# A fixed opening order laid out anew: fourth unit's scores earlier, two units' exponentials in a row, keys and values loaded per unit

## The chip, the core and the metric

The kernel runs on one core of one Trainium2 chip. A core has five engines that work side by side, each through its own queue in order: TensorE (matrix products; PE in the profile, PEld its weight loads), VectorE (DVE), ScalarE (ACT), GpSimd (POOL) and SyncE (SP), which here issues most DMA transfers. The metric is the device time of one execution in microseconds (us). The kernel before has a median of 1154.69 us over three runs (1153.79 to 1156.12).

## What is computed

Attention in chunks over 4 batches, 8 heads, 768 positions and 64 features per head, followed by two dense blocks over the 3072 tokens of 512 features, all in float32:

```python
for c in range(nc):                       # chunks of 32 queries
    k_full = concat(mem_k, k[c_start-16 : c_end+8])
    v_full = concat(mem_v, v[c_start-16 : c_end+8])
    a = exp(scale * q_c @ k_full.T - max)
    out[c] = (a / (sum(a) + 1e-9)) @ v_full
x = out as 3072 x 512
h = x @ w_in                               # 512 -> 2048
x = maximum(0.01 * h, h) @ w_out           # 2048 -> 512
return ((x @ w_a) * (x @ w_b)) @ w_out2    # 512 -> 1536 -> 512
```

## The kernel before

**Attention units.** Attention is cut into 24 units of 128 tokens (`UT`), six per batch. A unit goes through: `a_scores` (32 small products on TensorE, line 267), `a_max` (VectorE: row maxima, and for most units the subtraction), `a_exp` (ScalarE; for units 2 and 3, `by_scalar`, eight instructions that also sum), `a_soft2` (VectorE: division by the sum), `a_turn_mm` and `a_turn_copy` (transposes on TensorE, copies on ScalarE), `a_pv` (32 small products with V on TensorE, line 375) and `a_out` (ScalarE writes a rounded part `xh`, VectorE the remainder `xl`, the two halves of the split that gives float32 accuracy). Keys and values come by `k_load` and `v_load` (lines 251 and 259), two DMA transfers of 256 KB per unit, four buffers each.

**Weights.** `w_in` and `w_out` come as 16 column blocks and 16 row blocks. `order` is the list in which they are prepared: (0,0), (1,0), (2,0), (0,1), (3,0), (1,1), (4,0), (2,1) and so on, where (f,0) is a block of `w_in` and (f,1) one of `w_out`. Each entry goes through `Weights`: `load` (DMA of 512 KB), `bias` (ScalarE, line 103), `join` (three VectorE instructions, lines 113, 116 and 119), `cast` (ScalarE, line 173) and `low` (VectorE, line 182). `step` does one join, the biases of two later entries and the low part of the entry before.

**First dense block.** Tokens are taken in six blocks of 512. For a column block f, `mm1` (lines 412 to 414, tile `h`) multiplies x by (f,0), ScalarE applies the leaky rectifier (`g`) and rounds (`gh`), VectorE takes the remainder (`gl`); `mm2` (lines 532 to 536, tile `a`) multiplies by (f,1), two column blocks behind. For the first token block the first three column blocks (`LEAD`) are done on the first 256 tokens only (units 0 and 1), so that TensorE can begin before units 2 and 3 are ready; from f = 3 on all 512 tokens are taken.

**The order.** `InOrder` (line 31) wraps the engines: each instruction emitted through `pe`, `dve`, `act` or `sp` is put behind the one emitted before it on the same engine. So the opening, from the first load to the end of `first_items` (line 580), is an order written out by hand, in the sequence of the source. At its end `e.on = False` is set for all four wrappers, and from there on the framework's scheduler orders instructions by priority and its own estimate of when they are ready; instructions emitted through `nc.scalar` and the like are free from the start. In the profile the instructions of the written order carry line 44 or 47, the wrapper's; the free ones carry their own lines, and they may slip in among the others.

## Time and profile before

| what | us |
|---|---|
| median of three runs | 1154.69 |
| the profiled execution | 1154.32 |
| its span, first to last instruction | 1152.5 |
| TensorE busy in it | 1134.1 |
| VectorE busy | 665.4 |
| ScalarE busy | 441.7 |

The page's busy line gives each engine's share of the span, the table of stretches the same for parts of it, with the granted TensorE clock (1.00 is the level of 2.4 GHz, 0.50 that of 1.2 GHz) and the share of the time in which the 16 DMA engines worked. In a timeline a row has start, duration, engine, source line, operation, the tiles written and read, shapes, and in brackets the idle time of the engine before it with what ended it.

### The profile page before, as it was taken

What the parts mean: (1) busy time and instruction counts of PE and PEld (TensorE: products, weight loads), DVE (VectorE), ACT (ScalarE), POOL (GpSimd) and SP (SyncE); (2) the same over time, 40 slices, a digit from 0 to 9 for tenths busy, and PEclk for the clock granted to TensorE, in tenths of its full rate; (3) what the DMA queues carried; (4) which work ended last, traced back from release to release, by engine and by line L of the source; (5) the groups of instructions that cost most, each with busy time, mean ns of one, the idle gap of its engine ahead of it and who ended that gap; (6) DMA issues with size and microseconds to landing.
All of it is one profiled execution on the core that took longest, in us unless ns stands there. A gap on an engine that the chain in (4) does not pass through costs nothing.

```text
span 1152.5 us, 16036 instructions
## 1 busy us (share of the span) xinstructions
PE 1134.1 (98%) x6344; PEld 938.6 (81%) x6344; DVE 665.4 (58%) x1233; ACT 441.7 (38%) x734; POOL 6.3 (1%) x16
## 2 busy tenths in 40 slices
PE   6899999999999999999999999999999999999998
PEld 6678888888888888888888888888888888888887
DVE  6899489889979834545114433475433465433443
ACT  5787564556455534325223222241222232122210
POOL 2000000000000000000000000000000000000000
PEclk9999999999999999999999999999999999999999
DMA  9977899998999845336248335355544344443413
GB/s 325 354 264 279 308 341 322 317 354 300 330 339 333 298 164 182 111 114 215 92 146 314 144 128 201 128 227 220 208 148 163 146 148 187 185 166 142 186 64 110
DMA packets 68299, 250.67 MB, mean 217 GB/s; under 512 B 7297, under 2 KB 8705, under 8 KB 62849
## 3 DMA queue, kind: packets, MB, share of 16 engines
q1 hardware_dynamic: 67920, 249.33, 60.3%
q8 instruction: 50, 0.82, 0.3%
q10 hardware_dynamic: 304, 0.33, 0.1%
q14 instruction: 25, 0.20, 0.1%
HBM read 200.34 MB, written 49.28 MB: 217 GB/s over the span
## 4 chain that ended last, share of the span: by engine, by line
PE 94%; DVE 0%; DVEq 0%; issue 0%
PE h L412 7%; PE a L532 7%; PE a L536 7%; PE a L535 7%; PE h L414 7%; PE h L413 7%; PE o L925 6%; PE o L927 6%; PE o L926 6%; PE A L860 4%; PE A L859 4%; PE A L858 4%; PE C L858 3%; PE C L860 3%; PE C L859 3%; PE pv L385 2%
## 5 line engine op out<-in xcount | busy, mean ns | idle before, releaser
L412 PE MATMUL h<-xh,w 128*128 128x512 f32 (+1 forms) x384 | 152.1, 396 | 3.1 <-ACT w L47 3.1
L532 PE MATMUL a<-gh,w 128*128 128x512 f32 (+1 forms) x392 | 150.7, 385 | 0.9 <-DVE w L182 0.9
L535 PE MATMUL a<-gl,w 128*128 128x512 f32 (+1 forms) x392 | 150.4, 384 | 0.0
L536 PE MATMUL a<-gh,w 128*128 128x512 f32 (+1 forms) x392 | 150.4, 384 | 0.0
L413 PE MATMUL h<-xl,w 128*128 128x512 f32 (+1 forms) x384 | 149.0, 388 | 0.0
L414 PE MATMUL h<-xh,w 128*128 128x512 f32 (+1 forms) x384 | 148.9, 388 | 0.0
L430 DVE TENSOR_TENSOR gl<-g,gh 128x512 fp32r<-128x512 f32 (+1 forms) x96 | 65.4, 682 | 105.8 <-ACT gh L429 105.6
L925 PE MATMUL o<-w,cl 128*128 128x512 f32 x288 | 112.1, 389 | 0.0
L927 PE MATMUL o<-w,ch 128*128 128x512 f32 x288 | 112.0, 389 | 0.0
L926 PE MATMUL o<-w,ch 128*128 128x512 f32 x288 | 112.0, 389 | 0.0
L514 ACT ACTIVATE g<-h 128x512 f32<-128x512 f32 (+1 forms) x96 | 56.5, 589 | 126.3 <-PE h L414 125.5
L872 ACT COPY u<-A 128x512 f32<-128x512 f32 x72 | 42.3, 588 | 142.2 <-PE A L860 142.2
L412 PEld LDWEIGHTS h<-xh,w 128*128 128x128 f32 x384 | 72.5, 189 | 18.7 <-ACT w L47 3.2
L532 PEld LDWEIGHTS a<-gh,w 128*128 128x128 f32 x392 | 73.7, 188 | 16.3 <-DVE w L182 1.3
L880 DVE TENSOR_TENSOR ga<-u,C 128x512 f32<-128x512 f32 x36 | 24.8, 688 | 106.9 <-ACT u L872 77.7
L536 PEld LDWEIGHTS a<-gh,w 128*128 128x128 f32 x392 | 73.6, 188 | 14.5
L535 PEld LDWEIGHTS a<-gl,w 128*128 128x128 f32 x392 | 73.7, 188 | 14.5
L414 PEld LDWEIGHTS h<-xh,w 128*128 128x128 f32 x384 | 72.4, 189 | 14.8
L859 PE MATMUL A<-cl,wab 128*128 128x512 f32 x216 | 84.1, 389 | 0.0
L858 PE MATMUL A<-ch,wab 128*128 128x512 f32 x216 | 84.0, 389 | 0.0
L860 PE MATMUL A<-ch,wab 128*128 128x512 f32 x216 | 84.0, 389 | 0.0
L413 PEld LDWEIGHTS h<-xl,w 128*128 128x128 f32 x384 | 72.6, 189 | 14.1 <-DVE xl L47 0.3
(138 smaller groups left out, 1918.7 us busy)
## 6 DMA issues: line engine op xcount, KB each, us to landing
wab<-wab SPq DMA_DIRECT2D x36, 1792.0 KB, 7.4
w<-wod SPq DMA_DIRECT2D x116, 512.0 KB, 5.2
raw<-w SPq DMA_DIRECT2D x68, 512.0 KB, 6.9
k<-kl SPq DMA_DIRECT2D x48, 256.0 KB, 5.4
v<-vl SPq DMA_DIRECT2D x48, 256.0 KB, 5.4
wab<-pwb SPq DMA_DIRECT2D x12, 1024.0 KB, 7.7
wab<-pwa SPq DMA_DIRECT2D x12, 768.0 KB, 7.2
wod<-w SPq DMA_DIRECT2D x16, 512.0 KB, 6.1
```

The lines of the kernel that those rows point to most:

```text
L412: pe.matmul(ps, w[1], x[0], start=first, stop=False)
L413: pe.matmul(ps, w[0], x[1], start=False, stop=False)
L414: pe.matmul(ps, w[0], x[0], start=False, stop=last)
L532: pe.matmul(ps, slot[:, 1, c], gh[:, t], start=f == 0 and o == 0, stop=False, **kw)
L535: pe.matmul(ps, slot[:, 0, c], gl[:, t], start=False, stop=False, **kw)
L536: pe.matmul(ps, slot[:, 0, c], gh[:, t], start=False, stop=f == NF1 - 1 or (o == HALF and f == LEAD - 1), **kw)
L858: nc.tensor.matmul(ps, w[:, 1, i, c], hi[:, kc], start=first and kc == 0, stop=False, **kw)
L859: nc.tensor.matmul(ps, w[:, 0, i, c], lo[:, kc], start=False, stop=False, **kw)
L860: nc.tensor.matmul(ps, w[:, 0, i, c], hi[:, kc], start=False, stop=kc == HC - 1, **kw)
L925: nc.tensor.matmul(o, cl[:, q], w[:, 0, :], start=k == 0, stop=False)
L926: nc.tensor.matmul(o, ch[:, q], w[:, 1, :], start=False, stop=False)
L927: nc.tensor.matmul(o, ch[:, q], w[:, 0, :], start=False, stop=k == NCH - 1)
```

## The change

Keys and values of a unit come in one transfer of 512 KB each, with two buffers instead of four. The first unit's keys are issued first on SP, and the query halves of the first two units are spread over the queues of ScalarE and SP. `W1.load(7)` becomes `W1.load(6)` ahead of the fourth unit's values. In the written order: the cast of entry 1 goes behind the bias of entry 2; `a_scores(3)` comes from behind the first `mm1` and bias group to right behind `a_pv(1)`; `a_exp(3)` follows `a_exp(2)` with one bias between; the first `mm1` group is emitted ahead of all that `first_items` does, its `g` far later, behind both units' turned copies; both turns come together; `g1`, `join` of entry 5 and `g2` come behind the low part of entry 4; `a_turn_mm(3)` uses the `ps_a` pool. ScalarE stays in the written order through the first `W1.step()` of the loop.

```diff
--- before.py
+++ after.py
@@ -228,9 +228,9 @@
         while loaded[0] < min(upto, NU):
             u = loaded[0]
             if u < len(qs):
-                eng = act if u < 2 else sp
-                sp.dma_start(out=qs[u][0:64, 0:CH, :], in_=q_l[u, 0:64])
-                eng.dma_start(out=qs[u][64:128, CH:2 * CH, :], in_=q_l[u, 64:128])
+                first, second = ((act, sp), (sp, act), (sp, sp))[min(u, 2)]
+                first.dma_start(out=qs[u][0:64, 0:CH, :], in_=q_l[u, 0:64])
+                second.dma_start(out=qs[u][64:128, CH:2 * CH, :], in_=q_l[u, 64:128])
             else:
                 t = ap_.tile([P, CH, 16], F32, tag="qr", name="qr", bufs=2)
                 sp.dma_start(out=t, in_=q_l[u])
@@ -249,26 +249,27 @@
         copy(qb[64:128, :, CH:2 * CH], t[64:128])
 
     def k_load(upto):
-        while loaded[1] < min(upto, 2 * NU):
-            u, cp = divmod(loaded[1], 2)
-            t = ap_.tile([P, 512], F32, tag="k", name="k")
-            sp.dma_start(out=t, in_=k_l[u, cp])
-            kt[u, cp] = t
+        while loaded[1] < min(upto, NU):
+            u = loaded[1]
+            t = ap_.tile([P, 2, 512], F32, tag="k", name="k", bufs=2)
+            sp.dma_start(out=t, in_=k_l[u].rearrange("c p n -> p c n"))
+            kt[u] = t
             loaded[1] += 1
 
     def v_load(upto):
-        while loaded[2] < min(upto, 2 * NU):
-            u, cp = divmod(loaded[2], 2)
-            t = ap_.tile([P, 512], F32, tag="v", name="v")
-            sp.dma_start(out=t, in_=v_l[u, cp])
-            vt[u, cp] = t
+        while loaded[2] < min(upto, NU):
+            u = loaded[2]
+            t = ap_.tile([P, 2, 512], F32, tag="v", name="v", bufs=2)
+            sp.dma_start(out=t, in_=v_l[u].rearrange("c p n -> p c n"))
+            vt[u] = t
             loaded[2] += 1
 
     def a_scores(u):
         qb = q_of(u)
         s = ps_s.tile([P, 8, 64], F32, tag="s", name="s")
+        kk = kt.pop(u)
         for cp in range(2):
-            k = kt.pop((u, cp))
+            k = kk[:, cp]
             for hp in range(4):
                 for cpar in range(2):
                     o = (2 * cp + cpar) * 4 + hp
@@ -375,8 +376,9 @@
     def a_pv(u, pool, tag):
         pt = PT[u % 2]
         o = pool.tile([P, KC, UT], F32, tag=tag, name="pv")
+        vv = vt.pop(u)
         for cp in range(2):
-            v = vt.pop((u, cp))
+            v = vv[:, cp]
             for pair in range(2):
                 for cpar in range(2):
                     for hpar in range(2):
@@ -440,13 +442,13 @@
     W1 = Weights(order)
 
     x_tiles(("x", 0))
+    k_load(1)
     q_load(1)
     k_load(2)
     q_load(2)
-    k_load(4)
     act.dma_start(out=ident, in_=id_l)
     W1.load(1)
-    v_load(2)
+    v_load(1)
     W1.load(2)
     q_load(3)
 
@@ -459,11 +461,11 @@
     a_scores(0)
     a_scores(1)
     fill(6)
-    k_load(6)
-    v_load(4)
+    k_load(3)
+    v_load(2)
     W1.load(3)
     q_load(4)
-    k_load(8)
+    k_load(4)
     W1.load(5)
     a_max(0)
     a_exp(0)
@@ -477,8 +479,8 @@
     a_turn_copy(0, (1,))
     W1.bias(2)
     a_pv(0, ps_h, "h")
-    v_load(6)
-    W1.load(7)
+    v_load(3)
+    W1.load(6)
     W1.join(0)
     a_soft2(1)
     W1.join(1)
@@ -487,16 +489,18 @@
     a_scores(2)
     a_turn_copy(1)
     W1.join()
+    W1.cast(1)
+    W1.low(1)
+    W1.bias(3)
+    a_max(2)
     W1.cast(2)
-    W1.low(1)
-    a_max(2)
-    W1.bias(3)
     a_pv(1, ps_h, "h")
-    v_load(8)
+    v_load(4)
     W1.load(11)
     a_out(1, ("x", 0), UT)
     W1.low(2)
     a_exp(2)
+    a_scores(3)
 
 
     acc = {}
@@ -572,54 +576,51 @@
         if u > 3:
             q_place(u + 1, nc.scalar.copy)
         q_load(u + 3)
-        k_load(2 * u + 6)
+        k_load(u + 3)
 
     def load_v(u):
-        v_load(2 * u + 6)
+        v_load(u + 3)
 
     def first_items():
         parts = [items[f][2] for f in range(LEAD)]
+        h0 = mm1_pe(0, parts[0])
+        a_max(3)
+        a_soft2(2)
+        W1.bias(4)
+        a_exp(3)
         W1.join()
-        a_soft2(2)
-        h0 = mm1_pe(0, parts[0])
-        g0 = mm1_act(*h0)
-        W1.bias(4)
-        W1.cast(3)
-        W1.bias(5)
-        a_scores(3)
-        a_max(3)
-        W1.low(3)
+        h1 = mm1_pe(0, parts[1])
         a_turn_mm(2, ps_a, "a")
         a_turn_copy(2)
-        a_exp(3)
-        h1 = mm1_pe(0, parts[1])
+        W1.cast(3)
+        a_soft2(3)
+        a_turn_mm(3, ps_a, "a")
         a_pv(2, ps_s, "s")
         W1.join()
+        W1.low(3)
+        a_turn_copy(3)
+        g0 = mm1_act(*h0)
+        W1.bias(5)
+        W1.low(4)
+        h2 = mm1_pe(0, parts[2])
+        a_pv(3, ps_s, "s")
         W1.join()
-        W1.cast(4)
-        a_soft2(3)
-        W1.low(4)
         a_out(2, ("x", 0), 2 * UT)
+        mm2(0, parts[0], g0)
+        a_out(3, ("x", 0), 3 * UT)
+        W1.low(5)
         load_qk(2)
         W1.load(12)
         load_v(2)
         W1.load(13)
         g1 = mm1_act(*h1)
-        h2 = mm1_pe(0, parts[2])
-        a_turn_mm(3, ps_s, "s")
-        mm2(0, parts[0], g0)
-        a_turn_copy(3)
-        W1.cast(5)
         W1.bias(6)
         W1.join()
-        a_pv(3, ps_s, "s")
-        W1.low(5)
-        a_out(3, ("x", 0), 3 * UT)
         g2 = mm1_act(*h2)
         load_qk(3)
         load_v(3)
         W1.low(6)
-        for e in (pe, dve, act, sp):
+        for e in (pe, dve, sp):
             e.on = False
         return [(0, parts[1], g1), (0, parts[2], g2)]
 
@@ -796,6 +797,7 @@
         if first:
             W1.load(2 * f + 14)
             W1.step()
+            act.on = False
         behind.append((bi, parts, mm1(bi, parts)))
         if first:
             W1.step()
```

## Rows read from the trace of the kernel before

**Rows 1.** The page's busy line: us, share of the span, instructions.
```profile
PE 1134.1 (98%) x6344; PEld 938.6 (81%) x6344; DVE 665.4 (58%) x1233; ACT 441.7 (38%) x734; POOL 6.3 (1%) x16
```
**Rows 2.** Stretches: length, busy PE, PEld, DVE, ACT, POOL, clock, DMA share, GB/s.
```profile
8.00:20.00 12.00, 10.66 (x162) 9.79 (x160) 10.30 (x21) 6.17 (x11) 0.00 (x0) 1.00 1.04 339
20.00:38.00 18.00, 12.38 (x168) 11.03 (x164) 15.36 (x32) 17.16 (x56) 0.00 (x0) 1.00 0.97 375
38.00:66.00 28.00, 26.24 (x145) 21.10 (x145) 25.46 (x49) 20.39 (x32) 0.00 (x0) 0.94 0.77 277
66.00:112.00 46.00, 46.00 (x313) 37.79 (x314) 44.90 (x87) 36.21 (x60) 0.00 (x0) 1.00 0.88 310
```
**Rows 3.** TensorE's waits: two rows from 8 to 66 us, then after 66.
```profile
PE h L412 <- ACT w L47: 3.1, 1, 3.1
...
PE a L532 <- DVE w L182: 0.9, 2, 0.5
...
PE a L532 <- DVE w L182: 0.5, 1, 0.5
```
**Rows 4.** Timeline of the first 10 us: scores behind the keys, first maximum.
```profile
7.36 3.17 PE L47 MATMUL s<-k,qs 128*64 128x64 f32 x48 [0.23 <-DMA k<-kl]
...
8.56 0.69 DVE L47 TENSOR_REDUCE m<-s 128x8 f32<-128x512 f32 x1 [6.62 <-PE s L47]
```
**Rows 5.** Tile k: issue to landing, first unit's keys, then the fourth unit's.
```profile
DMA to landing us min/median/max: 4.4/4.7/5.1
...
DMA to landing us min/median/max: 6.1/6.1/6.1
```
**Rows 6.** Timeline from 15 to 31 us, some rows.
```profile
15.45 1.00 SPq L47 DMA_DIRECT2D k<-kl  x2
...
22.39 0.68 DVE L47 TENSOR_TENSOR w<-z,w 128x512 fp32r<-128x512 f32 x1
...
24.02 2.00 PE L47 MATMUL s<-k,qs 128*64 128x64 f32 x32
24.13 0.39 ACT L47 ACTIVATE g<-h 128x256 f32<-128x256 f32 x1
...
27.93 0.32 ACT L47 ACTIVATE p<-s,m 128x64 f32<-128x64 f32 x1
...
30.27 0.66 ACT L47 CAST w<-z 128x512 fp32r<-128x512 f32 x1
```
**Rows 7.** Timeline from 31 to 39 us: ScalarE's, VectorE's, TensorE's rows.
```profile
31.53 0.72 ACT L103 ACTIVATE raw<-raw 128x512 f32<-128x512 f32 x1
...
32.42 0.63 PE L47 MATMUL pT<-id,p 128*128 128x128 f32 x4 [1.59 <-DVE p L47]
...
33.08 1.18 ACT L47 COPY pt<-pT 64x512 f32<-64x512 f32 x2 [0.54 <-PE pT L47]
...
35.52 0.43 DVE L47 TENSOR_SCALAR z<-raw 128x512 int32<-128x512 int32 x1 [1.72 <-ACT raw L47]
...
37.41 0.68 DVE L47 SCALAR_TENSOR_TENSOR z<-raw,z 128x512 int32<-128x512 int32 x1
38.01 0.69 DVE L47 TENSOR_TENSOR w<-z,w 128x512 fp32r<-128x512 f32 x1
38.13 0.62 ACT L47 CAST w<-z 128x512 fp32r<-128x512 f32 x1 [0.15 <-DVE z L47]
```
**Rows 8.** Timeline from 38 to 45 us: first 512-wide products and the copies.
```profile
38.84 0.77 PE L412 MATMUL h<-xh,w 128*128 128x512 f32 x1 [3.14 <-ACT w L47]
...
43.20 0.28 PE L532 MATMUL a<-gh,w 128*128 128x256 f32 x1
...
44.56 1.11 ACT L248 COPY qz<-qr 64x512 f32<-64x512 f32 x1
44.63 0.40 PE L412 MATMUL h<-xh,w 128*128 128x512 f32 x1
```
**Rows 9.** A stretch, columns as in rows 2.
```profile
38.61:42.02 3.41, 3.18 (x7) 2.46 (x8) 3.41 (x9) 1.92 (x4) 0.00 (x0) 0.50 0.96 347
```

## The prediction

> **What bounds the kernel now.** I read the page's busy line first, then a table of stretches, then TensorE's waits, then the rows of the start in order of time. The busy line gives TensorE 1134.1 of 1152.5 us [rows 1], so 18.4 us of idle time is all that a new order can win. The stretches say where it lies: from 66 to 112 us TensorE is busy 46.00 of 46.00 us, while from 20 to 38 us it is busy 12.38 of 18.00 with ScalarE at 17.16 and VectorE at 15.36, and from 38 to 66 us 26.24 of 28.00 with VectorE at 25.46 [rows 2]. TensorE's waits after 66 us hold one entry, 0.5 us [rows 3], ahead of the group that starts at 65.96, on that very edge. So the end moves with the moment at which TensorE passes 66 us, and behind it nothing can be won. The start is an alternation of ScalarE and VectorE in a fixed order; its dearest wait is 3.1 us ahead of the first 512-wide product [rows 3]. I call that product step 3, its successor step 4 (TensorE's `h` groups), and the second-layer groups between them a1 and a2. I call the n-th entry of `order`, counted from 0, piece n. Step 3 needs piece 4, a1 piece 5, step 4 piece 6, a2 piece 7.
>
> **Prices.** VectorE takes 0.43 + 2 x 0.68 = 1.79 us for the three instructions that join a piece and 0.69 for its low part [rows 7]. ScalarE takes 0.72 for a bias and 0.62 for a cast [rows 7], 0.39 for `g` of a half block and as much for `gh`, 0.8 in all, and 30.27 - 27.93 = 2.34 for the eight exponentials of a unit [rows 6]. None of these is added or removed; all are moved.
>
> **Keys and values per unit.** The halves of the first unit's keys landed 4.4 and 5.1 us after their issue, and the scores went on at 7.36 behind the second one [rows 4, 5]. VectorE's first maximum came at 8.56 [rows 4]. Now one transfer of 512 KB is issued first, and no score starts before all of it is there. Full scores cost 2.00 us [rows 6], half of which used to run before 7.36. If the whole lands at 6.6 us (0.7 before the second half did, since one 128 KB transfer less is ahead of it) the maximum starts at about 8.75, 0.2 later. The bounds are 5.1 us (the first half's 4.4 us behind an issue at 0.74) and 8.0 us (0.7 behind the second half), so the shift lies between -1.3 and +1.6. I book it at nothing: the next step waits for a later transfer and has 1.3 us to cover it. Later units load the same bytes as early as before, where TensorE waits for no transfer.
>
> **Fourth unit's scores behind the second's products with V.** Before, they ran at 24.02, after the first product; now they stand ahead of it. They need the fourth unit's keys: two transfers issued from 15.45 to 16.45 that took 6.1 us each, so the second landed at about 22.2 [rows 5, 6]. TensorE, free after the second unit's products, waits until then and finishes at 24.3. That costs TensorE nothing lasting (scores and first product only change places), but VectorE's next instruction in the fixed order is now the maximum of these scores. It ended its low part at 23.07 [rows 6] and used to go on with a join; now it stands for 24.3 - 23.0 = 1.3 us, with all its joins behind it. That is a wait added.
>
> **VectorE up to step 3.** From 24.3: maximum 0.8, third unit's softmax 1.05 (one instruction of a low part's size and two short ones), join 1.8, fourth unit's softmax 1.05, join 1.8, low part 0.6 come to 31.4. (These are the starts' distances, a little under the durations, since neighbours overlap.) The next low part, of piece 3, waits for ScalarE, whose two new neighbours, the exponentials of both units, are done at 27.7; fourth softmax ends at 29.1, then transposes 0.63, their copies 1.18 [rows 7], `g` and `gh` 0.8, bias 0.72 and cast 0.62 give 33.05. With it join 4 ends at 33.05 + 0.6 + 1.8 = 35.5; two low parts of x and that of piece 4 follow at 0.6 each, the last ends at 37.3, and step 3 starts there. Before, it was held until 38.70 by the same low part [rows 7], which stood behind a join that waited 1.72 us for a bias. Step 3 is thus **1.5 us earlier**. What made room is that `gl` of the second step and join 5 now come after piece 4.
>
> **Clock.** Step 3 ran at half clock: between 38.61 and 42.02 the granted clock was 0.50, with 3.18 us busy [rows 9], behind the idle time of 3.14 us [rows 8]; at the full clock that work takes half, 1.6 us. In the walk TensorE's idle time ahead of step 3 is cut into 1.4, 0.8 and 1.6 us, and I take full clock: **1.6 us more**. TensorE could start a1 at 43.20 - 1.5 - 1.6 = 40.1 [rows 8].
>
> **Where these 3 us go.** What was moved behind piece 4 is now late. ScalarE stays in written order through the first step of the loop, so that the biases that slipped in at 31.53 and later (L103) [rows 7] now stand behind the cast of piece 5. From join 4's end the two engines hand one thing back and forth: cast 0.62, `g` and `gh` 0.80, bias 5 0.72, join 5 1.79, cast 5 0.62, bias 6 0.72, join 6 1.79, cast 6 0.62, low part 0.69: 8.3 us after 0.1 for overlaps, with nothing beside it. Piece 6 is there at 35.5 + 8.3 = 43.8 at the earliest. If VectorE slips the joins of pieces 7 and 8 between (1.0), `gl` of step 3 (0.6) and ScalarE one free bias (0.6), it is 46.0. Middle 45.0, so step 4 starts at 45.0 against 44.63 [rows 8]: **+0.4**; TensorE waits some 2 us ahead of it.
>
> **Behind step 4.** Before, a2 waited 0.4 us (two waits make 0.9 us, the later one 0.5 [rows 3]) for piece 7, whose cast stood behind two copies of 1.11 us [rows 8]; now step 4's own lateness covers piece 7: **-0.4**. The wait of 0.5 us at 65.96 goes with it if VectorE's order holds: -0.5. The SP queue sees the same bytes; `W1.load(6)` puts one piece behind the fourth unit's values, a piece that is not touched before 35 us. Sum: +0.4 - 0.4 - 0.5 = **-0.5 us**. The profiled execution took 1154.32 us (its span is 1152.5, with 1.8 around it), 0.4 under the median, so the forecast is 1153.8.
>
> **A rule against the row.** DMA moved 375 GB/s from 20 to 38 us at a share of 0.97, and 339 GB/s from 8 to 20 us at a share of 1.04 [rows 2]: full either way, at two rates, the lower one where the 128 KB query transfers lie. The Trainium skill (Perfetto Trace Analysis, DMA Optimizations) says that larger transfers use HBM's bandwidth better, and also that splitting lets some work start sooner when DMA engines are idle. By the first, the fourth keys would come sooner; by the second, the split would only have helped in the first microseconds. Without the page: at 375 instead of 339 GB/s the 12 us shrink by 1.15 and the keys land at 21.0. That belongs to the first rival.
>
> **Rivals.** First, *the lead is kept*: the keys land 0.9 to 1.15 us sooner, VectorE's added wait shrinks as much, and nothing slips into the chain, so that step 4 starts at 43.9 - 0.9 = 43.0 (-1.6), a2 and the group at 65.96 wait no more (-0.9): -2.5, 1151.8. For it speaks that the free biases are held back by the written order; against it that VectorE's order behind the first step is free.
>
> Second, *slower, by the alternation*: ScalarE's two free copies into `qz` (2 x 1.11 [rows 8]) are put ahead of cast 5 or 6, in the gap in which ScalarE waits for a join. Step 4 then starts at 46.0 + 1.8 = 47.8 (+3.2), TensorE stands for over 4 us before it, longer than the 3.14 that went ahead of the half clock, and pays 1.6 once more; a2's and the last wait (0.9) are absorbed: +3.9, 1158.2. It decides once step 4 starts behind 46.5.
>
> Third, *the first transfer is late*: keys of 512 KB land at 8 us, every queue shifts by 1.5, 1.3 of it is covered by the wait for the fourth keys, or, if those are as late, none: up to +1.0 in all, 1155.3.
>
> Fourth, *the edit does not do what it says*: the exponentials do not follow each other since the scores come too late; then ScalarE stands for as long as the fourth keys are later than 23 us, and the sum stays within 1 us of the forecast. It is in the forecast's own spread, 1152.4 to 1155.3 (the chain's 8.3 to 10.5 us).
>
> **How the numbers follow.** Forecast 0.44, lead kept 0.28, slower by the alternation 0.18, first transfer late 0.10. About 0.2% (2.3 us) is what a measurement of this kernel can tell from no change. Faster by more is the first rival alone, 0.28; slower by more the second, 0.18; the rest, 0.54, is within. The range leaves out the outer half of either rival's spread: 1151.3 to 1157.6.
>
> **What would show it.** Right: VectorE idle by about 1.3 us ahead of the fourth unit's maximum near 24 us; eight and eight exponentials with one bias between; step 3 near 37.3 at a clock of 1.00; then a wait of about 2 us ahead of step 4, released by a low part; TensorE passing its 66 us mark within 1.5 us of before. Wrong: fourth keys landing by 21 us; the `qz` copies ahead of cast 6; a clock of 0.50 between 42 and 48 us; a wait of TensorE behind 66 us.

## The result and the profile after

The changed kernel takes 1163.37 us (median of seven executions, 1156.86 to 1163.9) against 1154.69 (1153.05 to 1156.12 on that chip): 1.0062 times the time before by all the executions, 95% interval 1.0042 to 1.0083 (the two medians alone give 1.0075). The forecast was 1153.8, in a range of 1151.3 to 1157.6. The execution whose trace was taken is the quickest of the seven, 1156.86 us with a span of 1154.9, so the trace of after shows only some 2 of the 9 us. Two further traces of the same kernel, `after_again` and `after_third`, stand below and show the rest.

The page's busy line of the kernel after, which answers to [rows 1]:

```profile
PE 1132.7 (98%) x6344; PEld 938.0 (81%) x6344; DVE 665.9 (58%) x1233; ACT 439.8 (38%) x734; POOL 6.3 (1%) x16
```

TensorE is busy 1.4 us less than before, in a span that is 2.4 us longer. The stretches, columns as in [rows 2], with one more behind them:

```profile
8.00:20.00 12.00, 10.68 (x162) 9.94 (x160) 10.50 (x21) 6.63 (x12) 0.00 (x0) 1.00 1.04 358
20.00:38.00 18.00, 13.98 (x171) 12.50 (x167) 15.80 (x32) 15.44 (x53) 0.00 (x0) 1.00 1.03 362
38.00:66.00 28.00, 22.27 (x131) 17.81 (x130) 25.04 (x48) 21.46 (x35) 0.00 (x0) 1.00 0.75 278
66.00:112.00 46.00, 46.00 (x318) 38.05 (x318) 45.26 (x88) 35.34 (x59) 0.00 (x0) 1.00 0.90 322
112.00:330.00 218.00, 216.98 (x1501) 179.71 (x1500) 182.08 (x394) 116.85 (x191) 0.00 (x0) 1.00 0.90 319
```

Up to 38 us TensorE has done 1.6 us more than before. From 38 to 66 it is busy 22.27 us where it was 26.24: some 1.6 us of the difference is the half clock of step 3 that is gone (the clock is 1.00 now), the rest is work not done, since TensorE stood idle. From 112 to 330 us, where the kernel before is busy all the time, 1.0 of 218 us is idle. The waits of TensorE, first from 8 to 66 us, then behind 66, answer to [rows 3]:

```profile
PE s L277 <- issue: 3.5, 1, 3.5
PE h L414 <- DVE w L182: 1.8, 1, 1.8
...
PE h L414 <- DVE w L47: 1.4, 1, 1.4
...
PE h L415 <- DVE xl L401: 0.9, 2, 0.5
PE A L860 <- DMA wab<-wab: 0.4, 1, 0.4
PE a L536 <- ACT x L553: 0.2, 1, 0.2
```

The 3.1 us ahead of step 3 have shrunk to 1.4; a wait of 3.5 has come ahead of step 4, one of 1.8 later, and behind 66 us there are three small kinds (L415, L860, L536) that the kernel before does not have; its one wait there, 0.5 at 65.96, is gone. The order of events, from the timeline from 20 to 67 us of the kernel after (start, duration, engine, line, operation; idle time before it in brackets), which answers to [rows 6 to 8]:

```profile
20.52 1.75 PE L47 MATMUL s<-k,qs 128*64 128x64 f32 x26 [0.23 <-PE pv L47]
21.27 0.31 ACT L47 ACTIVATE p<-s,m 128x64 f32<-128x64 f32 x1
23.07 0.69 DVE L47 TENSOR_REDUCE m<-s 128x8 f32<-128x512 f32 x1 [0.60 <-PE s L47]
...
36.20 0.47 PE L414 MATMUL h<-xh,w 128*128 128x512 f32 x1 [1.45 <-DVE w L47]
...
38.74 1.79 ACT L47 ACTIVATE raw<-raw 128x512 f32<-128x512 f32 x3
39.62 0.38 PE L536 MATMUL a<-gh,w 128*128 128x256 f32 x1 [0.43 <-DVE w L47]
...
41.98 0.62 ACT L173 CAST w<-z 128x512 fp32r<-128x512 f32 x1
42.50 1.08 ACT L248 COPY qz<-qr 64x512 f32<-64x512 f32 x1
43.33 0.68 DVE L182 TENSOR_TENSOR w<-z,w 128x512 fp32r<-128x512 f32 x1
43.59 1.08 ACT L249 COPY qz<-qr 64x512 f32<-64x512 f32 x1
44.77 0.53 PE L277 MATMUL s<-k,qz 128*64 128x64 f32 x10 [3.46 <-issue]
45.23 0.50 PE L414 MATMUL h<-xh,w 128*128 128x512 f32 x1
...
63.87 0.50 PE L414 MATMUL h<-xh,w 128*128 128x512 f32 x1 [1.84 <-DVE w L182]
```

Step 3 starts at 36.20 (38.84 before), a1 at 39.62 (43.20 before). Then three biases stand in a row on ScalarE, the cast of piece 6 comes at 41.98, its low part ends at 44.01, and the two copies into `qz` (L248, L249) hold ScalarE until 44.67. Ten matrix products of the fifth unit's scores (L277) stand ahead of step 4 in TensorE's queue and read `qz`: they start at 44.77, step 4 at 45.23.

**The rest of the 9 us.** `after_third` has the same order and the same two waits; two stretches of it, columns as above:

```profile
46.04:52.86 6.82, 6.31 (x24) 5.06 (x25) 5.07 (x10) 2.23 (x4) 0.00 (x0) 0.50 1.03 410
...
69.93:73.34 3.41, 3.41 (x10) 2.62 (x9) 3.41 (x7) 1.05 (x2) 0.00 (x0) 0.50 0.91 342
```

The granted clock is 0.50 through step 4 and again behind the second wait, 10.2 us in all. In the first trace of after it stayed at 1.00 behind waits of the same length. To price the half clock, here are the stretches from the start of a1 to the start of the eighth second-layer group, 245 products each (24 spare ones, as the trace counts them, come on top in the last): the first trace of after, `after_again`, `after_third`, and `after_fill14`, a kernel of the same order with spare products in the first wait, which stands below:

```profile
39.62:80.34 40.72, 35.42 (x245) 29.00 (x245) 38.06 (x71) 32.19 (x52) 0.00 (x0) 1.00 0.81 295
40.70:85.53 44.83, 39.51 (x245) 32.00 (x245) 38.26 (x71) 32.18 (x52) 0.00 (x0) 0.89 0.77 275
41.40:86.62 45.22, 39.91 (x245) 32.28 (x245) 38.24 (x71) 32.17 (x52) 0.00 (x0) 0.89 0.74 272
40.83:83.26 42.43, 39.53 (x269) 32.60 (x268) 38.18 (x71) 32.23 (x52) 0.00 (x0) 0.96 0.82 290
```

The waits of the first three are the same, and the way takes 40.7 us with no half clock, 42.4 with the second fall alone and 44.8 and 45.2 with both: the first fall costs 2.4 to 2.8 us, the second 1.7. It shows as busy time of TensorE (39.91 us for the products that took 35.42), not as idle time.

Of fifteen executions of the kernel after, two had a mean clock of 1.000 and took 1156.9 and 1157.7 us, one had 0.997 and took 1160.5, and twelve had 0.994 to 0.996 and took 1162.6 to 1168.5. That is more than the falls cost up to the eighth group; in the two of the twelve that were traced the waits behind it are longer too (below).

### The profile page after: what moved, and what is told of

Its sections match the earlier page's. It is cut to its first block, busy times and chain, and to the rows that moved or that the text cites. A ratio compares the mean times of both kernels' runs of the same rounds, so it can differ in the third digit from the quotient of the medians.

```text
span 1154.9 us, 15958 instructions
## 1 busy us (share of the span) xinstructions
PE 1132.7 (98%) x6344; PEld 938.0 (81%) x6344; DVE 665.9 (58%) x1233; ACT 439.8 (38%) x734; POOL 6.3 (1%) x16
## 4 chain that ended last, share of the span: by engine, by line
PE 71%; DMA 1%; DVE 0%; issue 0%; DVEq 0%
PE o L927 6%; PE o L929 6%; PE o L928 6%; PE A L860 4%; PE A L862 4%; PE A L861 4%; PE a L536 4%; PE h L414 4%; PE a L539 4%; PE a L540 4%; PE h L415 4%; PE h L416 4%; PE C L860 3%; PE C L862 3%; PE C L861 3%; PE B L860 1%
## 5 line engine op out<-in xcount | busy, mean ns | idle before, releaser
L536 PE MATMUL a<-gh,w 128*128 128x512 f32 (+1 forms) x392 | 150.6, 384 | 0.6 <-DVE w L47 0.4
L415 PE MATMUL h<-xl,w 128*128 128x512 f32 (+1 forms) x384 | 148.6, 387 | 0.9 <-DVE xl L401 0.9
L536 PEld LDWEIGHTS a<-gh,w 128*128 128x128 f32 x392 | 73.6, 188 | 15.8 <-DVE w L47 0.9
L860 PE MATMUL A<-ch,wab 128*128 128x512 f32 x216 | 84.1, 389 | 0.4 <-DMA wab<-wab 0.4
L415 PEld LDWEIGHTS h<-xl,w 128*128 128x128 f32 x384 | 72.2, 188 | 15.2 <-DVE xl L401 1.6
```

The source lines that it names most:

```text
L415: pe.matmul(ps, w[0], x[1], start=False, stop=False)
L536: pe.matmul(ps, slot[:, 1, c], gh[:, t], start=f == 0 and o == 0, stop=False, **kw)
L860: nc.tensor.matmul(ps, w[:, 1, i, c], hi[:, kc], start=first and kc == 0, stop=False, **kw)
```

## The experiments

All comparisons are with the kernel before on the same chip. To set traces beside each other I read three marks from each: the start of the first products with V, the start of the eighth second-layer group (79.70 us before), and the end of TensorE's last product. The table gives, in us more than the kernel before, the start (first mark), the way from the first to the second mark, and from the second to the last. The start differs from one execution to the next with the landing of the first transfers (in `after_again` and `after_third` TensorE stands 1.8 and 1.9 us for query halves between their first products, in the first trace of after not at all). The other two depend on the kernel, but not on it alone, as the three traces of after show. The half clock column lists stretches at 0.50 up to 160 us; the kernel before has one, 38.6 to 42.0.

| kernel | ratio (95% interval) | start | to 8th group | behind it | half clock, us |
|---|---|---|---|---|---|
| after | 1.0062 (1.0042 to 1.0083) | +0.1 | +0.5 | +1.8 | none |
| after_again | 1.0093 (1.0076 to 1.0110) | +1.2 | +4.6 | +4.9 | 44.4 to 51.2, 68.3 to 71.7 |
| after_third | 1.0063 (1.0040 to 1.0085) | +1.9 | +5.0 | +4.3 | 46.0 to 52.9, 69.9 to 73.3 |
| a_act_free (not held) | 1.0002 (0.9992 to 1.0011) | +0.9 | -2.1 | +1.9 | none |
| a_kv_halves (order, hold) | 1.0067 (1.0047 to 1.0087) | +0.4 | +5.1 | +6.0 | 29.8 to 36.6, 46.9 to 50.3, 67.4 to 70.8 |
| a_order_only | 1.0020 (1.0010 to 1.0029) | +1.6 | -1.6 | +3.3 | none |
| b_kv_unit (loads) | 1.0038 (1.0023 to 1.0052) | +0.5 | +0.7 | +1.9 | 23.2 to 26.6, 40.3 to 43.7 |
| b_act_held (hold) | 1.0002 (0.9993 to 1.0011) | -0.2 | +2.0 | +0.5 | 22.5 to 25.9, 39.6 to 43.0 |
| b_kv_held (loads, hold) | 1.0031 (1.0019 to 1.0043) | +1.7 | -0.5 | +1.5 | 25.5 to 29.0, 39.2 to 42.6 |
| after_fill | 1.0019 (1.0007 to 1.0030) | +2.0 | -0.4 | +5.2 | none (one at 346) |
| after_s4_late | 1.0052 (1.0039 to 1.0065) | +0.2 | +0.8 | +3.9 | 43.4 to 50.3 |
| after_fill14 | 1.0057 (1.0043 to 1.0071) | +1.3 | +2.2 | +3.7 | 65.9 to 69.3 |
| after_fill18 | 1.0044 (1.0028 to 1.0059) | +1.2 | +2.6 | +5.3 | 23.9 to 27.3, 153.6 to 157.0 |
| b_fill | 0.9998 (0.9989 to 1.0006) | +1.1 | -1.4 | 0.0 | none |
| b_kv_fill | 1.0039 (1.0025 to 1.0052) | +2.0 | -0.7 | +4.1 | none |
| a_copy_dve | 1.0009 (0.9998 to 1.0019) | +1.5 | -0.2 | +0.3 | 44.6 to 48.0 |
| after_copy | 1.0077 (1.0062 to 1.0092) | +2.6 | +5.0 | +3.7 | 46.7 to 53.5, 70.6 to 74.0 |
| a_order_copy | 1.0023 (1.0012 to 1.0034) | +0.1 | -0.1 | +2.1 | 28.3 to 31.7, 42.0 to 45.4 |

### Which part of the change costs

The change has three parts that can be undone one by one: the loads (keys and values per unit, with the query transfers spread otherwise and `W1.load(6)`), the order of the first steps, and the hold (ScalarE kept in written order through the loop's first step). The new places of the first transfers were not taken apart: they stand with the loads in `b_kv_unit` and `b_kv_held`, and with the order in `a_kv_halves` and `a_order_only`, where only the halves come back.

**after_again**: the kernel after, unchanged.

> The changed kernel once more, for the trace of an ordinary execution: the traced one took 1156.9 us at a mean granted clock of 1.000, six others 1160.5 to 1163.9 us at 0.995 to 0.997. Theory C (clock): the new idle time ahead of step 4 (3.5 us in the trace) lets the granted clock fall to 0.50 in most executions; then 1160 to 1164 us, and the trace shows two or three stretches of about 3.4 us at 0.50 between 40 and 75 us, with TensorE's waits little changed. Theory L (loads): keys and values as one transfer land late in most executions; then the clock is as in the traced one and the waits for transfers are longer.

1165.16 us (1164.65 to 1168.52). The order of the instructions on every engine and both waits are those of the first trace (3.47 and 1.85 us), the half clock is new, and the waits behind the eighth group add up to 3.9 us (1.5 in the first trace).

**a_kv_halves**: keys and values of the kernel after in halves again; the order of the first transfers and the hold stay.

```diff
-            t = ap_.tile([P, 2, 512], F32, tag="k", name="k", bufs=2)
-            sp.dma_start(out=t, in_=k_l[u].rearrange("c p n -> p c n"))
+            t = ap_.tile([P, 512], F32, tag="k", name="k")
+            sp.dma_start(out=t, in_=k_l[u, cp])
...
```

> The changed kernel with keys and values loaded in halves again, four buffers each, the written order as in the changed one. Theory L: back to 1153 to 1157 us. Theory C: only if the idle time ahead of step 4 changes; as that comes from the order of ScalarE and VectorE, 1160 to 1164 us.

1162.33 us: nothing comes back. The loads are not what makes the kernel after slow. Nor can the half clock be all of it: two of the four executions had a mean clock of 0.999 and still took 1161.1 us.

**a_act_free**: ScalarE freed at the end of the first steps, as before.

```diff
-        for e in (pe, dve, sp):
+        for e in (pe, dve, act, sp):
             e.on = False
...
-            act.on = False
```

> The changed kernel with ScalarE set free at the end of the opening as before, not after the first step of the loop. Theory A (alternation): the biases of pieces 6 to 8 slip forward, piece 6 is there 1 to 2 us sooner, step 4 starts at 43 to 44 us, the clock does not fall, and the time is 1153 to 1156 us. If the hold of ScalarE is not what makes piece 6 late, it stays at 1160 to 1164 us.

1154.96 us: the whole loss is gone. Its stretch from 38 to 66 us, and two of TensorE's waits behind 34 us:

```profile
38.00:66.00 28.00, 24.52 (x144) 19.93 (x143) 27.02 (x52) 21.05 (x35) 0.00 (x0) 1.00 0.84 322
```

```profile
PE a L536 <- DVE w L47: 2.0, 1, 2.0
...
PE s L277 <- issue: 0.7, 1, 0.7
```

VectorE is busy 27.02 of 28 us where the kernel after has 25.04. Between the joins, ScalarE now slips the biases of later pieces (L103) wherever it would wait. (Both kernels run six biases between 32 and 44 us; `a_act_free` is through with them at 39.2, the kernel after has four of them left at 38.7, ahead of the cast of piece 6 and the copies into `qz`.) VectorE's waits from 32 to 66 us, all for casts, roundings and exponentials of ScalarE, fall from 3.5 to 1.7 us. At TensorE one long wait becomes two short ones: counted from the first products with V, a1 starts 1.6 us later than in the kernel after, behind the cast of piece 5, which comes 1.5 us later, and the fifth unit's scores start 1.2 us earlier. It waits 2.0 us ahead of a1 and 0.7 ahead of the scores instead of 0.4 and 3.5, and stands 2.1 us ahead of the kernel before at the eighth group instead of 0.5 behind it.

**b_kv_unit**: the kernel before with the loads alone.

```diff
-            t = ap_.tile([P, 512], F32, tag="k", name="k")
-            sp.dma_start(out=t, in_=k_l[u, cp])
+            t = ap_.tile([P, 2, 512], F32, tag="k", name="k", bufs=2)
+            sp.dma_start(out=t, in_=k_l[u].rearrange("c p n -> p c n"))
...
```

> The kernel before with one part of the change alone: keys and values per unit, first keys first, query halves spread as in the change; the written order of the engines as before. Theory C and theory A: 1153 to 1156 us, as the order of ScalarE and VectorE is untouched. Theory L: 1158 us or more.

1159.1 us: alone, the loads cost 0.38%.

**b_act_held**: the kernel before with the hold alone.

```diff
-        for e in (pe, dve, act, sp):
+        for e in (pe, dve, sp):
...
+            act.on = False
```

> The kernel before with one line changed: ScalarE stays in written order through the first step of the loop, as in the kernel after, while loads, scores and exponentials stay as before. Theory of the hold: this alone gives a wait of TensorE of 2 to 3.5 us ahead of step 4 and a later one near 64 us, and 1160 to 1164. Theory of the new order (exponentials in a row and the fourth scores' place bring it): the hold alone costs under 1.5 us, 1154 to 1156.

1155.36 us, ratio 1.0002: alone, the hold costs nothing that can be measured. The theory of the hold alone has fallen. TensorE waits 1.2 us ahead of step 4, since step 3 came at 38.81 there and not at 36.20, and a1 at 43.53 and not at 39.62. (The traced execution is the slowest of the ten; it has one half clock more than the kernel before, from 22.5 us.)

**a_order_only** (`a_act_free` with the edit of `a_kv_halves`) and **b_kv_held** (`b_kv_unit` with the edit of `b_act_held`) are the two combinations left.

> The kernel after with ScalarE freed at the end of the first steps as in the kernel before, and keys and values in halves: of the change, the order of the first steps (and the first transfers' places) alone. If the three parts simply add up (loads per unit +4.3 us alone; order and loads together without the hold +0.3), the order alone is worth -4: 1151. If the loads per unit cost only in the order of before, by one more half clock there: 1153.5 to 1155.5, with no half clock before 100 us, step 3 near 37 and 1 to 2 us of late waits.

> The kernel before with keys and values per unit and with ScalarE held through the first step of the loop: two of the three parts, the order of the first steps as before. If the parts add up (loads +4.3, hold +0.2): 1159 to 1160. If hold and loads make each other dearer, as hold and order do: 1162 to 1165. If what the loads cost is the re-dealing of the free part, a new deal may as well cost nothing: 1155 to 1157.

1156.36 and 1157.38 us. Neither sum holds: the parts don't add up. (Three measurements of the kernel after lie up to 0.3% apart, so the small differences should not be read closely.) In per cent above the kernel before: loads 0.38, order 0.20, hold 0.02; loads and hold 0.31, order and loads 0.02; order and hold 0.67, all three 0.62 to 0.93. The one large loss appears where order and hold meet, with the loads or without. In the traces, what the order gives TensorE at step 3, the hold turns into a wait ahead of step 4: 3.5 us in the kernel after and in `a_kv_halves`, 0.7 in `a_act_free` and `a_order_only`.

### What the wait ahead of step 4 costs

**after_fill**: 13 spare products behind a1 (`after_mm2()` holds them behind its last product).

```diff
+            if bi == 0 and f == 3:
+                spare = ps_h.tile([P, TB], F32, tag="h", name="spare")
+                with after_mm2():
+                    for _ in range(13):
+                        nc.tensor.matmul(spare[:, 0:P], ident, ident, start=True, stop=True)
```

**after_s4_late**: only the fifth unit's scores held back, no spare work.

```diff
-            at(bi, f, a_scores, u)
+            at(bi, f, late_scores if u == 4 else a_scores, u)
```

> The kernel after with 13 spare products of 128 columns (the unit matrix by itself, into a tile that nobody reads) issued behind a1, so that TensorE has about 2.8 us of work in the 3.5 us in which it waits ahead of step 4; the scheduler then also puts the fifth unit's scores behind step 4. Clock theory: what the change costs above the 1156.9 us of its traced execution is the granted clock of 0.50 that follows these 3.5 us; with them filled there is no half clock behind 44 us (none between 44 and 72), step 4 still starts between 43.5 and 46, and the time is 1156 to 1159. Theory of the hold alone (ScalarE in written order makes step 4 and the following groups late, whatever the clock): half clock or not, the time stays at 1162 to 1166. If the loads per unit are the cause: no change either, 1162 to 1166.

> The kernel after with the fifth unit's scores held behind the second-layer group that is emitted before them and nothing else; no spare work. It is the counterpart of the fill: the wait ahead of step 4 stays at 2 to 3 us (for the cast and the low part of piece 6), the wait near 64 us at 1 to 2 us. Clock theory: the clock falls to 0.50 behind one of these waits, 1160 to 1165. Theory that the hoisted scores themselves make step 4 late (they wait for the two copies into qz): step 4 starts 0.6 to 1 us earlier and the time falls to 1158 to 1160 without any filling.

1157.09 and 1161.02 us. Both change the order that the scheduler deals, too. With the scores out of the way step 4 starts 28.5 us behind the first products with V, 1.2 earlier than in after, so the scores did delay it; the half clock comes all the same (43.4 to 50.3). With the wait filled there is no half clock there and the time lies 4 us lower. But the clock is not shown to be what makes these 4 us: of the four executions of `after_s4_late`, two with a mean clock of 0.998 and 0.999 took 1161.0 us and the traced one, with 0.996, took 1159.3.

**after_fill14** is the cleaner pair to after: 14 spare products around a1, and all other instructions in their places on every engine.

```diff
+            if bi == 0 and f == 3:
+                spare = ps_h.tile([P, TB], F32, tag="h", name="spare")
+                for _ in range(14):
+                    nc.tensor.matmul(spare[:, 0:P], ident, ident, start=True, stop=True)
```

> The kernel after with 14 spare products of 128 columns (the unit matrix by itself, into a tile that nobody reads) around a1, and the order of every other instruction on every engine as in the kernel after: 3 of them ahead of a1, 11 in the 3.5 us in which TensorE waits ahead of step 4 for the copies into qz. Clock theory: the clock stays at 1.00 through step 4 (no half clock between 44 and 52), a1 and step 4 start where they did, and the time is 1156 to 1159.5, against 1163 to 1165 of the kernel after. Theory that the late waits behind 130 us, and not the clock, carry the loss: they stay, and so does the time, 1162 to 1165.

Two stretches of its trace, step 4 and then the place behind the second wait:

```profile
46.50:53.30 6.80, 6.80 (x46) 5.76 (x45) 6.69 (x12) 3.97 (x8) 0.00 (x0) 1.00 1.03 421
65.92:69.34 3.42, 3.42 (x9) 2.65 (x9) 3.42 (x7) 1.01 (x2) 0.00 (x0) 0.50 0.79 280
```

Step 4 runs at full clock as the clock theory said; behind the second wait, which was not filled, the clock falls. In the traces the fall that is gone is worth 2.4 to 2.8 us up to the eighth group (42.4 us from a1 against 44.8 and 45.2 with both falls). The time, 1161.09 (1158.44 to 1162.27), lies between the two expectations, but its interval (1.0043 to 1.0071) overlaps that of after, so the timed pair does not show the part by itself.

**after_fill18** fills some of the second wait as well; **after_third** is the kernel after beside it.

```diff
+            if bi == 0 and f == 6:
+                spare = ps_h.tile([P, TB], F32, tag="h", name="spare")
+                for _ in range(4):
+                    nc.tensor.matmul(spare[:, 0:P], ident, ident, start=True, stop=True)
```

> The kernel after with 14 spare products of 128 columns around a1 and 4 more in TensorE's second wait (1.8 us ahead of the group that started at 63.87 in the kernel after); every other instruction keeps its place on its engine. With the first wait filled the half clock moved behind the second one (65.92 to 69.34). Clock theory: now there is none before 100 us, the fifth second-layer group starts 1.6 us earlier than with 14 products alone, and the time is 1158 to 1160 (1161.1 with 14 products). Theory that the late waits carry what is left: 1160.5 to 1162, clock or not.

> The kernel after, unchanged, beside the one with 18 spare products on the same chip: it prices the clock by the difference of the two. Clock theory: 1162 to 1166 with a mean granted clock of 0.995 to 0.997, that is 3 to 6 us above the filled one. Theory of the late waits: within 2 us of the filled one.

1160.73 (1159.26 to 1163.59) and 1163.23 (1157.66 to 1165.7): 2.5 us apart, with much spread and overlapping intervals. In the trace of `after_fill18` the clock stayed at 1.00 from 27.3 to 153.6 us, and still the kernel lies 0.44% above the one before, since its late waits are there (5.3 us behind the eighth group, one half clock among them). From a1 to the eighth group it takes 40.8 us, as the first trace of after does without a half clock. Three executions with a clock of 1.000 took 1159.3 to 1161.3, and the two of the kernel after with that clock 1156.9 and 1157.7: at full clock the filled kernel is the slower one, and why is open. So the clock is a part, shown in the traces up to the eighth group, and both theories hold some of the loss.

**b_fill**: the kernel before with 12 spare products in the 3.1 us ahead of step 3.

```diff
+        spare = ps_h.tile([P, TB], F32, tag="h", name="spare")
+        for _ in range(12):
+            pe.matmul(spare[:, 0:P], ident, ident, start=True, stop=True)
```

> The kernel before with 12 spare products of 128 columns (the unit matrix by itself, into a tile that nobody reads) behind the fourth unit's products with V, in the 3.1 us in which TensorE waits ahead of step 3. Clock theory: step 3 then runs at full clock instead of 0.50 (3.41 us at half clock, worth 1.6 us), and the kernel takes 1152.5 to 1153.7 (ratio 0.998 to 0.999), unless the gain is lost ahead of step 4. Rival: the clock at step 3 does not hang on TensorE's idle time: half clock near 38.6 us as before, ratio 0.999 to 1.001.

Step 3 of its trace, from its start to the start of a1:

```profile
39.76:42.90 3.14, 3.10 (x12) 2.33 (x13) 3.14 (x7) 1.66 (x3) 0.00 (x0) 1.00 1.01 373
```

The clock is 1.00 where [rows 9] has 0.50. From step 3 to a1 it is 3.2 us instead of 4.4, and the eighth group comes 1.4 us earlier, counted from the first products with V. The time is 1154.52 against 1154.98: the interval reaches from 1.3 us faster to 0.7 slower. A gain is not shown, so this is no version that beats the kernel before.

**b_kv_fill**: `b_kv_unit` with 6 and 13 spare products in its two idle stretches.

```diff
     a_pv(1, ps_h, "h")
+    fill(6)
...
         a_pv(3, ps_s, "s")
+        spare = ps_h.tile([P, TB], F32, tag="h", name="spare")
+        for _ in range(13):
+            pe.matmul(spare[:, 0:P], ident, ident, start=True, stop=True)
```

> The kernel before with keys and values per unit, and spare products of 128 columns in two idle stretches of TensorE: 6 behind the second unit's products with V (ahead of the first product of W1) and 13 ahead of step 3. Loads alone took 1159.1 with two stretches of half clock (23.2 to 26.6 and 40.3 to 43.7). Clock theory: both go, each worth 1.6 us: 1155.5 to 1157. If the loads cost by their late waits and the later first scores instead: 1157.5 to 1159.5, whatever the clock.

1159.24 us, as without them, though the clock was 1.00 throughout the start. Here the clock is not what the loads cost: the way to the eighth group got 1.4 us shorter, but the first products with V came later and the late waits grew.

### The late waits

**a_copy_dve**: `a_act_free` with the copies that empty the second-layer sums given to VectorE from the second block on; TensorE's order is the same.

```diff
-                    act.copy(y[:, t], ps)
+                    (act.copy if bi == 0 else dve.tensor_copy)(y[:, t], ps)
```

Its ground is this chain on the timeline of `a_act_free` from 336 to 341 us:

```profile
338.04 0.62 ACT L125 CAST pw<-pz 128x512 fp32r<-128x512 f32 x1 [1.85 <-DMA wab<-pwa]
...
339.06 0.58 ACT L553 COPY x<-a 128x512 f32<-128x512 f32 x1
...
339.69 0.50 PE L536 MATMUL a<-gh,w 128*128 128x512 f32 x1 [1.40 <-ACT x L553]
```

A cast (L125) for the next weights waits 1.85 us on ScalarE for its buffer to be stored; the copy (L553) that empties a sum stands behind it, and TensorE waits 1.40 us for that copy.

> The kernel after with ScalarE freed as in the kernel before (1155.0 so far), and the copies of the second-layer sums from the second block on given to VectorE instead of ScalarE; TensorE's order does not change, nor any engine's before 130 us. Theory that the late wait at 339.7 (1.4 us, behind a copy queued after a cast that waits for a buffer) is the scheduler's dealing of ScalarE's queue: it goes, the one near 648 (0.6 us, a transfer) stays, and the time is 1153.2 to 1154.2. Theory that something else is late there (the transfers themselves): the wait stays under another name, 1154.5 to 1155.5.

TensorE's only wait behind 66 us in its trace:

```profile
PE A L859 <- DVE gb L885: 0.9, 1, 0.9
```

The wait went, and the last column falls from 1.9 to 0.3. The time does not: 1155.68, ratio 1.0009. In this trace the start was 1.5 us late (0.9 in `a_act_free`) and a half clock came at 44.6, so the mechanism is shown in the trace and its worth is not.

**after_copy** (all such copies of the kernel after on VectorE) and **a_order_copy** (`a_order_only` with the edit of `a_copy_dve`). The edit of the first:

```diff
-                    act.copy(y[:, t], ps)
+                    dve.tensor_copy(y[:, t], ps)
```

> The kernel after, ScalarE held as there, with the copies of the second-layer sums (the first block's too) given to VectorE; TensorE's order does not change. Theory that three terms add up (start of the transfers, first 80 us with the clock, late waits behind ScalarE's queue): only the third changes, from 4 to 5 us (traces of the kernel after at a mean clock of 0.996) to under 1, and the time falls from 1163 to 1165 to 1159 to 1161. Theory that the late waits only shift to the next queue: within 1.5 us of the kernel after.

> The order of the first steps alone (keys and values in halves, ScalarE freed as before; 1156.4 so far) with the copies of the second-layer sums given to VectorE from the second block on; TensorE's order does not change. The trace of the order alone stood 1.6 us ahead of the kernel before in its 16th group of products, counted from its first products with V, and lost 3.2 us behind that. If the late term goes as it did with the loads per unit (1.8 to 0.3): 1153.5 to 1154.5, the one version that may lie below the kernel before. If not: 1155.5 to 1157.

1164.59 and 1158.13 us: no gain in either. TensorE's waits behind 100 us in `after_copy`:

```profile
PE A L860 <- DMA wab<-wab: 0.9, 1, 0.9
PE h L415 <- DVE xl L401: 0.9, 1, 0.9
PE h L414 <- ACT xh L400: 0.7, 1, 0.7
PE a L536 <- DVE x L553: 0.7, 2, 0.5
```

Where ScalarE had been held the waits moved to other names, as the rival said.

Why the kernel before, `b_fill` and (nearly) `b_act_held` have none, and every kernel with the new order or the new loads 0.3 to 6.0 us behind the eighth group, stays open. Most of these edits deal the part that the scheduler orders freely anew, but the order is not all of it: the three traces of after, `after_fill14` and `after_fill18` have one and the same order there on TensorE, VectorE, ScalarE and SyncE and lose 1.8, 4.9, 4.3, 3.7 and 5.3 us. The 1.8 belong to the trace that started earliest and had no half clock, so start and clock may each be behind it; `b_fill` has the order of the kernel before, started 1.1 us later, and lost nothing. I found no quantity in the traces that goes with it.

## Why the prediction was wrong, step by step

**Bound.** That the start decides was half right. That "behind it nothing can be won" was read off a kernel without waits there, and I took it to mean that nothing can be lost. In the kernel after 1.8 to 4.9 us are lost behind the eighth group. The sum had no term for it: the late waits are one of the two terms that it put at nothing without a reason, and their cause is open. Nor are 18.4 us of idle time all that an order can win or lose: the half clock lies in TensorE's busy time.

**Keys and values per unit**, booked at nothing: mis-sized. Alone they cost 0.38% (4.4 us), with the new order nothing (0.20 without them, 0.02 with them). The bound of the first transfer held: the first maximum came at 8.32, 0.2 earlier than in [rows 4], not 0.2 later. The price does not lie there, and `b_kv_fill` finds none of it in the clock; where it lies is open. Nor did the rate of the transfers tell the two apart: from 8 to 20 us the kernels with halves moved 339 [rows 2], 357 (`b_act_held`) and 370 GB/s (`b_fill`), those with whole units 358 (after), 365 (`b_kv_unit`) and 371 (`a_act_free`). The Trainium skill (Perfetto Trace Analysis, DMA Optimizations) has it that larger transfers use HBM's bandwidth better; at 256 against 512 KB no run here shows it.

**Fourth unit's scores**: the keys landed at 20.3, not at 22.2. The queue issued them at 13.0, 2.4 us earlier than in [rows 6]; "as early as before" was wrong. VectorE's wait was 0.60 us, not 1.3. This is the first rival's condition, and it was met.

**Step 3**: right in kind, short in size: 36.20 against 37.3. The lead over the kernel before is 2.6 us, not 1.5: the fourth unit's maximum started 1.2 us ahead of the forecast's 24.3, and step 3 1.1.

**Clock at step 3**: right, 1.00 in all three traces of after.

**The alternation**: step 4 at 45.23 against 45.0 (43.8 to 46.0), but by another last link: piece 6 was complete at 44.01, and then the hoisted scores waited for the `qz` copies. That was the second rival's mechanism at another place.

**The wait ahead of step 4**: this is the step that failed. I wrote "some 2 us". My own terms give more: a1 from 40.1, 1.7 us long (39.62 to 41.31 in the trace of after), ends at 41.8, and step 4 at 45.0 leaves 3.2. That is above the 3.14 us that went ahead of the half clock in the kernel before [rows 8], so by the same reasoning with which I took back 1.6 us at step 3 I should have paid them at step 4. (The 3.14 us are no limit: behind 1.84 us at 68.54 the clock fell in `after_third`, and behind 3.46 it held in the first trace.) I tied that price to the second rival instead, "once step 4 starts behind 46.5". The price had to hang on TensorE's wait, not on the moment at which step 4 starts: an earlier step 3 lengthens that wait. It was 3.46 us, with step 4 at 45.23, and the half clock behind it cost 2.4 to 2.8 us up to the eighth group in the two traces in which it came.

**The clock's price** was mis-sized as well: 1.6 us once. Between the first trace of after and `after_third`, with the same order and the same waits, it is 5.0 - 0.5 = 4.5 us up to the eighth group (4.1 with `after_again`), in two falls, 6.82 and 3.41 us long. The medians of `after_fill18` and `after_third` are 2.5 apart, in intervals that overlap.

**Behind step 4**: a2's wait and the one at 65.96 did go, as said (-0.9), but one of 1.84 us came at 63.87, also VectorE's low part, that I had not looked for.

**Rivals.** The second one (slower by the alternation, 1158.2, chance 0.18) named the right mechanism up to the eighth group: hold, copies, wait ahead of step 4, clock. Its price was 3.9 us against some 9, and it had no late waits either. "A clock of 0.50 between 42 and 48 us" and "a wait of TensorE behind 66 us" stood among the signs of a wrong forecast; both came.

The sum of the 9 us, from three traces of after: start 0.1 to 1.9, way to the eighth group 0.5 at full clock and 4.6 and 5.0 where the clock falls, behind the eighth group 1.8 to 4.9. That the hold is needed for the loss is shown by `a_act_free`, and the clock's part by the filled kernel of the same order; what makes the last term is open.

## What to carry to other kernels

Where a fixed order gives one engine a lead, work out the length of the next wait as the difference of two times that you have already written down; a lead that the next link can't use only makes that wait longer, and a wait of TensorE can cost behind it as well as in it (here 2.4 to 2.8 us behind 3.5, when the clock fell). An engine held in written order loses the work it slips in between, and the loss shows on the engine it feeds (here VectorE, 25.04 us busy against 27.02). A stretch without waits in the trace of before says nothing on what a new order will do there: book a loss on that side, since a change to a scheduled program can deal the rest of it anew, and since even one order lost 1.8 us there in one execution and 4.9 in another.

## What the runs showed of the hardware

The same waits don't always bring the clock down: behind 3.46 us of idle time it stayed at 1.00 in one trace of the kernel after, behind 3.47 us it fell to 0.50 for 6.8 us in two others. The first products with V, behind the same instructions, started at 15.54, 16.64 and 17.32 us in these three traces, by when the first transfers landed, so one trace of each of two kernels can't be compared to less than some 2 us at the start. And half clock that was taken away (step 3 of `b_fill`, 3.2 us for 4.4) was not seen in the time, whose interval reaches from 1.3 us faster to 0.7 slower.
